# First loads on another queue, and one shared place for the rows of conditional slots, in a fused attention and expert kernel

## The chip, the cores and the metric

The kernel runs on one core of a Trainium2 chip. The metric is device time in microseconds (us), lower is better. Before the change the median of six runs is 837.75 us (835.44 to 839.51).

The core has five engines, each with its own in-order instruction queue: TensorE (PE; its weight loads are shown as PEld), VectorE (DVE), ScalarE (ACT), GpSimd (POOL) and SyncE (SP). Transfers between HBM and on-chip memory are issued from the queues of SP, ACT or POOL and carried out by 16 DMA engines which all three share.

## The reference

The first part is an attention over short windows; its output, laid out as 4608 rows of 512, goes through a layer in which each row is given to one of eight experts.

```python
# attention: q, k, v of shape (8, 8, 576, 64); heads 0-3 plain, 4-7 dilated by 4
scores = scale * np.matmul(q, k.transpose(0, 1, 3, 2))
rel = pos[:, None] - pos[None, :]
mask_plain = (rel >= 0) & (rel < window)                       # window 32
mask_dil = (rel >= 0) & (rel < window * dilation) & (rel % dilation == 0)
scores = np.where(masks[None, :, :, :], scores, -1000000000.0)
scores = scores - np.max(scores, axis=-1, keepdims=True)
attn = np.exp(scores)
attn = attn / (np.sum(attn, axis=-1, keepdims=True) + 1e-09)
x = (attn @ v).transpose(0, 2, 1, 3).reshape(4608, 512)
# experts: w_gate (512, 8), w1 (8, 512, 1024), w2 (8, 1024, 512)
logits = x @ w_gate
expert_idx = np.argmax(logits, axis=1)
gate_w = softmax(logits)[np.arange(N), expert_idx]
# for the rows of expert e:
h = np.maximum(x_sorted[lo:hi] @ w1[e], 0.0)
y_sorted[lo:hi] = h @ w2[e]
out = gate_w[:, None] * y          # rows back in their first order
```

## The kernel before

**Attention** runs as 32 units: for each of the 8 batches, two kinds of heads (`ty` 0 plain, 1 dilated), and two pairs of heads (`hl`) of each kind. Unit 0 is batch 0, plain, first pair; units 0 and 1 use the plain heads' q and k, units 2 and 3 the dilated heads' (the last q and k load of a batch), unit 4 begins batch 1. A unit goes through these steps, pipelined over the units:

- `turn` (L297): PE transposes q and k of the unit (L315 for plain, L323 for dilated heads); VectorE evicts q with its scale, ACT copies k into `kT` (L308).
- `front` (L344): in the first four batches the masks enter by PE: four matmuls of the mask table against a 64x64 identity ("turn") put the mask values into the score banks (L352), and 36 matmuls of q and k add the scores on top (L364). VectorE takes the minima (L380). In later batches VectorE adds the masks ("add0", "add1") instead.
- `exponentials` (L397): ACT, 18 activations (L401). `norm` (L411): VectorE's reciprocal, and POOL's multiply of the whole unit (L416).
- `weights` (L420): PE transposes the weights, VectorE evicts. `summed` (L432): PE multiplies with v (L441). `row_part` (L523): PE transposes back into rows by `turner` (L534), which holds four copies of a 128x128 identity, each with 8 columns of `w_gate` beside it, so that the logits come with the transpose. POOL writes the token numbers into the rows from the constants `cst` (L527).

The `route` of a batch (L546) picks the experts and writes the batch's rows to a bucket in HBM by POOL's indirect DMAs (L227).

**The experts' part** (`moe`, L1092) goes over slots of up to 128 rows of one expert. A slot takes 64 matmuls with w1 (L1173), 16 with w2 (L1205), an eviction by ACT that scales by the gate weight (L1216), a copy of the rows' token numbers (L1219), and an indirect DMA by POOL to the output rows (`scatter`, L1222). 36 slots are sure (`SURE`); the 37th to the 41st (slots 36 to 40) run only if the routing needs them, each within a `tc.If` (L1122). Of these one runs with the data here. Slots are spread between the units of attention by a clock kept while the program is written, and fill the rest of the time alone.

The order on each engine is laid by a scheduler from modelled times; instructions of one engine may change places if their data allow it.

**The first loads.** SP's queue issues q of batch 0 (L255, L261), then v (L270 to L286), and, from L481 on, one write to the bucket and the loads of batch 1. ACT's queue issues an identity (L187), k of batch 0 in four pieces and one load for the dilated heads (L255, L261), and between the second and third k piece the table of all masks (`masks`, L257, 616 KB) and the constants (`cst`, L258, 165 KB); behind k come three more copies of the identity (L474) and `w_gate` (L475) for `turner`.

**The ends of the conditional slots.** `spare` (L1110 to L1116) gives each of the five conditional slots a place of its own for 128 rows and their token numbers. VectorE clears the rows and sets each token number to `NOWHERE`, which the indirect DMA drops. A slot that runs fills its place; behind all blocks (L1238 and after) five `scatter`s write all five places. The write of a sure slot waits in the list `late` until the next slot has made its first eviction.

Of the kernel before, what the change touches and what calls it, by code (L numbers as in the profile page):

```python
# [12 lines left out]
F32 = mybir.dt.float32  # L13
I32 = mybir.dt.int32
BF16 = mybir.dt.bfloat16
# [5 lines left out]
B, H, S, DH = 8, 8, 576, 64  # L21
WIN, DIL = 32, 4
STRIP = S // DIL
N, DM, E, F = B * S, H * DH, 8, 1024
# [11 lines left out]
QUARTER = DM // 4  # L36
# [24 lines left out]
NSLOT = _most_slots()  # L61
NROWS = E * CAP + 128
NOWHERE = 1.0e6
E1 = E + 1
SURE = N // 128
# [8 lines left out]
LAG = 2  # L74
# [9 lines left out]
def _constants():  # L84


    def band(j, ty):

        qi, ki = 64 * j + np.arange(64)[:, None], max(0, 64 * j - WIN) + np.arange(96)[None]
        seen = (qi - ki >= 0) & (qi - ki < WIN)  # L90
        if ty:
            seen &= qi // STRIP == ki // STRIP
        return np.where(seen, 0.0, BIG)

    def mask(ty):

        pairs = [(0, 1), (2, 3), (4, 5), (6, 7), (8, 8)]
        return np.concatenate([np.concatenate([band(j, ty) for j in two]) for two in pairs], 1)

    p = np.arange(128)  # L100
    e = np.arange(E)

    parts = {"add0": mask(0)[:, 0:384], "add1": mask(1)}
    for name, ty, js in (
        ("even0", 0, (0, 2, 4, 6, 8, 8)), ("even1", 1, (0, 2, 4, 6, 8)), ("odd1", 1, (1, 3, 5, 7, 8))
    ):
        parts[name] = np.tile(np.concatenate([band(j, ty) for j in js], 1), (2, 1))
    parts["turn"] = np.tile(np.eye(64), (2, 1))  # L110
    mask_at, n = {}, 0
    for name, a in parts.items():
        mask_at[name] = n
        n += a.shape[1]
    mask_at["odd0"] = mask_at["even0"] + 96
    exact = np.concatenate(list(parts.values()), 1).astype(np.float32).astype(ml_dtypes.bfloat16)
    parts = {
        "tri": np.triu(np.ones((128, 128)), 1)[:, :96],
        "ones": np.ones((128, 128)),
        "rev": np.tile(E - e, (128, 1)),  # L120
        "ecap": np.tile(e * CAP, (128, 1)),
        "tok": p[:, None] + TT * np.arange(NT)[None],
        "row": p[:, None],
        "eidx": np.tile(np.minimum(np.arange(E1), E - 1), (128, 1)),
        "twice": np.tile(2 * np.arange(NSLOT), (128, 1)),
    }
    parts["first"] = np.tile(np.append(np.arange(E)[::-1] / E, -1e6), (128, 1))

# [24 lines left out]
    last_at, k = {}, 0  # L153
    for name, a in last.items():
        last_at[name] = (k, a.size)
        k += a.size
    last = np.concatenate([a.reshape(1, -1) for a in last.values()], 1).astype(np.float32)
    return np.ascontiguousarray(np.concatenate(cols, 1)), at, np.ascontiguousarray(exact), mask_at, np.ascontiguousarray(last), last_at


@with_exitstack
def kernel(
# [10 lines left out]
    nc = tc.nc  # L173
    packed, at, exact, mask_at, packed_last, last_at = _constants()
# [10 lines left out]
    eye = nc.inline_tensor(np.eye(128, dtype=np.float32), name="c_id").ap()  # L185
    ident = turner[:, 0, 0:QUARTER]
    nc.scalar.dma_start(ident, eye)  # L187
    masks = cpool.tile([128, exact.shape[1]], BF16, name="masks")
    cst = cpool.tile([128, packed.shape[1]], F32, name="cst")

    before = cpool.tile([TT, B * NT + 1, E], F32, name="before")
# [6 lines left out]
    avail = cpool.tile([128, E1], F32, name="avail")  # L198
    nc.vector.memset(avail[:, E:E1], 4.0 * NSLOT)
    exs = cpool.tile([1, NSLOT], F32, name="exs")  # L200

    def const(name, rows=128):
        a, w = at[name]
# [46 lines left out]
    def load_qk(b, ty):  # L250
        for name, src, queue in (("q", q, nc.sync), ("k", k, nc.sync if b else nc.scalar)):
            if ty == 0:
                x = pool.tile([TT, NT, 4, DH], F32, tag=name + "0", name=f"{name}0_{b}", bufs=1)
                for h in range(4):
                    queue.dma_start(x[:, :, h, :], src[b, h].rearrange("(t p) d -> p t d", p=TT))  # L255
                    if (b, name, h) == (0, "k", 1):
                        queue.dma_start(masks, nc.inline_tensor(exact, name="c_mask").ap())  # L257
                        queue.dma_start(cst, nc.inline_tensor(packed, name="c_pack").ap())  # L258
            else:
                x = pool.tile([72, 4, 512], F32, tag=name + "1", name=f"{name}1_{b}", bufs=1)  # L260
                queue.dma_start(x, src[b, 4:8].rearrange("h (p x) d -> p h (x d)", p=72))  # L261
            t[b, name, ty] = x
# [81 lines left out]
    def front(qT, kT, ty, early):  # L344
# [3 lines left out]
        for r in range(2) if early else ():  # L348
            rows = slice(DH * r, DH * r + DH)
            for c in range(2):  # L350
                a, n = mask_at[("even", "odd")[c] + str(ty)], 480 if c == r else 384
                nc.tensor.matmul(  # L352
                    sc[r][64 * c : 64 * c + 64, 0:n],
                    lhsT=masks[rows, mask_at["turn"] : mask_at["turn"] + 64],
                    rhs=masks[rows, a : a + n],
                    start=True,
                    stop=False,
                )
# [19 lines left out]
        for i, n, p0, p1, s in places:  # L378
            if early:
                nc.vector.tensor_reduce(  # L380
                    out=lo[p0:p1, i : i + n], in_=s.rearrange("p (i k) -> p i k", k=96),
                    axis=AX, op=OP.min,
                )
            else:
                a = mask_at[f"add{ty}"] + 96 * (1 if (i, ty) == (4, 0) else i % 5)
                nc.vector.tensor_tensor(
                    out=e[p0:p1, i : i + n].rearrange("p i k -> p (i k)"),
                    in0=s,
                    in1=masks[p0:p1, a : a + 96 * n],
                    op=OP.add,  # L390
                )
        if not early:
# [74 lines left out]
    def attention():  # L467


        units = [(b, ty, hl) for b in range(B) for ty in range(2) for hl in range(2)]  # L470
        for ty in range(2):
            load_qk(0, ty)
        for c in range(1, 4):
            nc.scalar.dma_start(turner[:, c, 0:QUARTER], eye)  # L474
        nc.scalar.dma_start(  # L475
            turner[:, :, QUARTER:PART], moe_w_gate.rearrange("(c p) e -> p c e", p=128)
        )
        for ty in range(2):
# [613 lines left out]
    def moe():  # L1092
# [7 lines left out]
            nc.vector.tensor_copy(xt, ps)  # L1100
            return xt

        late, outs, spare = [], [], {}
        xt = None
        for j in range(NSLOT):
            if j == SURE:


                for i in range(SURE, NSLOT):
                    a = pool.tile([128, S], F32, tag="xT", name="spare", bufs=3) if i < SURE + 3 \  # L1110
                        else pool.tile([128, 9, 96], F32, tag="e", name="spare", bufs=LAG + 1)
                    if i >= SURE + 3:
                        a = a.rearrange("p i k -> p (i k)")
                    spare[i] = a[:, 0:DM], mpool.tile([128, 1], I32, name=f"to_{i}", bufs=1)
                    nc.vector.memset(spare[i][0], 0.0)
                    nc.vector.memset(spare[i][1], int(NOWHERE))  # L1116
            if j >= SURE:

                while late:
                    late.pop(0)()  # L1120
                guards.close()
                guards.enter_context(tc.If(live[0] > j))  # L1122
            x = xs[j]
            if xt is None:
                xt = across(j)
# [71 lines left out]
            for f in range(8):  # L1197
# [10 lines left out]
                    fetch()  # L1208
                if f < 7:
                    yield 0.88  # L1210
            if j >= SURE:
                y, to = spare[j]
            else:
                y = mpool.tile([128, DM], F32, tag="yo", name="y")
                to = mpool.tile([128, 1], I32, tag="to", name="to", bufs=6)
# [14 lines left out]
                tc.declare_no_dep(i, group="out", reason="no token is in two slots")  # L1230
                tc.add_to_no_dep_group("out", i)

            (late if j < SURE else outs).append(scatter)
            done[1] = 2 * j + 2
            fetch()
            xt = nxt
            yield 0.88
        guards.close()  # L1238
        for scatter in outs:
            scatter()  # L1240

# [85 lines left out]
```

## Time and profile before

The profiled execution took 839.54 us, with a span from first to last instruction of 837.8 us.

| | value |
|---|---|
| median of 6 runs | 837.75 us |
| the profiled execution, its span | 839.54 us, 837.8 us |
| PE busy | 768.6 us (92%) |
| VectorE, ACT, POOL busy | 288.9, 227.3, 147.6 us |
| mean granted clock of PE | 0.957 |
| DMA over the span | 196.89 MB, mean 235 GB/s |
| w1 matmuls (L1173), w2 matmuls (L1205) | 276.0, 255.1 us |
| last matmul ends, last eviction by ACT | 821.8, 822.5 us |

The profile's own page gives each engine's busy time, the span in 40 slices of 20.9 us, the chain of work that ended last, and groups of like instructions. In timelines a line holds start and duration in us, the engine (a "q" behind its name marks its sequencer, which issues DMAs and waits), the line of the kernel, the operation, what it writes and reads, how many, and in brackets how long the engine had been idle and what released it. Lines on one source line give counts, then shortest, median and longest duration in ns, then first and last start in us. Lines on waits give the total in us, how often, and the longest. A line for a window gives its bounds and length, each engine's busy us and count, PE's granted clock, the DMA engines' share, and GB/s.

### The profile page before, as it was taken

What the parts mean: (1) busy time and instruction counts of PE and PEld (TensorE: products, weight loads), DVE (VectorE), ACT (ScalarE), POOL (GpSimd) and SP (SyncE); (2) the same over time, 40 slices, a digit from 0 to 9 for tenths busy, and PEclk for the clock granted to TensorE, in tenths of its full rate; (3) what the DMA queues carried; (4) which work ended last, traced back from release to release, by engine and by line L of the source; (5) the groups of instructions that cost most, each with busy time, mean ns of one, the idle gap of its engine ahead of it and who ended that gap; (6) DMA issues with size and microseconds to landing.
All of it is one profiled execution on the core that took longest, in us unless ns stands there. A gap on an engine that the chain in (4) does not pass through costs nothing.

```text
span 837.8 us, 17999 instructions
## 1 busy us (share of the span) xinstructions
PE 768.6 (92%) x6822; PEld 588.3 (70%) x6822; DVE 288.9 (34%) x963; ACT 227.3 (27%) x853; POOL 147.6 (18%) x141
## 2 busy tenths in 40 slices
PE   2898888699999999989999998699999999999992
PEld 1787777677877777777777786486867465577770
DVE  1575857557434433443346224611110110101010
ACT  0875655353433233313333110000101001010000
POOL 0233243123121311141113004200000000000002
PEclk9997978899999999999999999699999999999996
DMA  9876669799998984889326728599994393983994
GB/s 202 174 140 166 139 179 385 194 241 293 310 335 259 361 205 151 287 303 276 122 69 211 261 96 291 187 325 320 322 341 144 118 306 110 326 310 128 321 331 161
DMA packets 166268, 196.89 MB, mean 235 GB/s; under 512 B 73569, under 2 KB 88033, under 8 KB 166179
## 3 DMA queue, kind: packets, MB, share of 16 engines
q1 hardware_dynamic: 153156, 169.45, 66.8%
q0 software_dynamic: 6992, 20.35, 6.5%
q10 hardware_dynamic: 6030, 5.89, 2.6%
q8 instruction: 57, 0.93, 0.5%
q14 instruction: 33, 0.26, 0.1%
HBM read 216.98 MB, written 23.33 MB: 287 GB/s over the span
## 4 chain that ended last, share of the span: by engine, by line
PE 85%; issue 4%; ACT 3%; DMA 2%; DVE 2%; SPq 1%; POOL 0%; POOLq 0%; ACTq 0%; DVEq 0%
PE ph L1173 30%; PE py L1205 28%; PE xrow L534 5%; PE xo L441 4%; PE weights L426 4%; PE scores L364 3%; DMA k<-in_k_dram 2%; PE turned L315 2%; PE xt L1098 2%; ACT e L401 2%; PE ph L1135 2%; PE py L1135 2%; PE turned L323 2%; SPq L255 1%; DVE lo L380 1%
## 5 line engine op out<-in xcount | busy, mean ns | idle before, releaser
L1173 PEld LDWEIGHTS ph<-xt,w 128*128 128x128 f32 x2240 | 266.3, 195 | 29.8 <-issue 29.4
L1173 PE MATMUL ph<-xt,w 128*128 128x128 f32 x2240 | 276.0, 279 | 12.2 <-issue 12.2
L1205 PE MATMUL py<-w,h 128*128 128x512 f32 x560 | 255.1, 598 | 0.0
L1205 PEld LDWEIGHTS py<-w,h 128*128 128x128 f32 x560 | 101.5, 191 | 101.9 <-issue 100.2
L1222 POOL DMA_INDIRECT out_dram<-y,to x36 | 35.7, 993 | 365.0 <-ACT y L1216 337.7
L1100 DVE COPY xt<-xt 128x512 f32<-128x512 f32 x38 | 26.2, 689 | 186.1 <-PE xt L1098 183.8
L416 POOL TENSOR_TENSOR e<-e,rec 128x864 f32<-128x864 f32 x32 | 52.4, 1639 | 184.1 <-DVE rec L415 127.9
L1216 ACT ACTIVATE y<-py,x 128x512 f32<-128x512 f32 x36 | 24.7, 686 | 218.0 <-PE py L1205 180.8
L227 POOL DMA_INDIRECT bucket<-rows,idx x48 | 44.6, 930 | 89.7 <-DVE idx L612 31.8
L428 DVE COPY eT<-weights 96x384 f32<-96x384 f32 x96 | 48.5, 547 | 29.6 <-PE weights L426 26.6
L401 ACT ACTIVATE e<-e,lo 128x96 f32<-128x96 f32 x144 | 51.8, 361 | 17.1 <-DVE lo L393 17.1
L1184 ACT ACTIVATE h<-ph 128x512 f32<-128x512 f32 x35 | 20.9, 596 | 127.2 <-PE ph L1173 84.3
L401 ACT ACTIVATE e<-scores,lo 128x96 f32<-128x96 f32 (+1 forms) x160 | 52.9, 344 | 5.0 <-DVE lo L380 2.2
L534 PE MATMUL xrow<-turner,xT 128*96 128x136 f32 x384 | 53.5, 292 | 0.0
L534 PEld LDWEIGHTS xrow<-turner,xT 128*96 128x96 f32 x384 | 49.6, 173 | 5.2 <-issue 4.1
L441 PE MATMUL xo<-eT,v 96*64 96x64 f32 (+1 forms) x1216 | 45.8, 228 | 5.2 <-issue 4.9
L441 PEld LDWEIGHTS xo<-eT,v 96*64 96x64 f32 x1216 | 40.2, 141 | 12.5 <-issue 6.3
L1193 DVE TENSOR_SCALAR h<-ph 128x512 f32<-128x512 f32 x35 | 24.1, 689 | 66.6 <-PE ph L1173 66.5
L426 PE MATMUL weights<-turner,e 128*96 128x128 f32 x288 | 42.7, 299 | 0.8 <-POOL e L416 0.8
L364 PEld LDWEIGHTS scores<-kT,qT 64*64 64x64 f32 x1152 | 30.5, 138 | 15.2 <-issue 6.6
L541 DVE COPY rows<-xrow 96x408 f32<-96x408 f32 x32 | 18.5, 577 | 64.7 <-PE xrow L534 61.4
L364 PE MATMUL scores<-kT,qT 64*64 64x96 f32 x1152 | 35.0, 254 | 5.4 <-ACT kT L308 4.5
(205 smaller groups left out, 594.6 us busy)
## 6 DMA issues: line engine op xcount, KB each, us to landing
w<-in_moe_w_dram SPq DMA_DIRECT2D x164, 1024.0 KB
x<-bucket SPq DMA_DIRECT2D x26, 273.0 KB
v<-in_v_dram SPq DMA_DIRECT2D x32, 192.0 KB
q<-in_q_dram SPq DMA_DIRECT2D x32, 144.0 KB
q<-in_q_dram SPq DMA_DIRECT2D x8, 576.0 KB
v<-in_v_dram SPq DMA_DIRECT2D x48, 96.0 KB
k<-in_k_dram SPq DMA_DIRECT2D x28, 144.0 KB
k<-in_k_dram SPq DMA_DIRECT2D x7, 576.0 KB
```

Source lines behind the costliest of these rows:

```text
L227: nc.gpsimd.indirect_dma_start(out=bucket, out_offset=bass.IndirectOffsetOnAxis(ap=idx, axis=0), in_=rows, in_offset=None, bounds_check=NR ...
L364: nc.tensor.matmul(sc[r][64 * c : 64 * c + 64, 96 * (i % 5) : 96 * (i % 5) + 96], lhsT=qT[rows, 64 * j : 64 * j + 64], rhs=kT[rows, first_ ...
L401: nc.scalar.activation(out=e[p0:p1, i], in_=s[:, 96 * (i - i0) : 96 * (i - i0) + 96], func=AF.Exp, bias=lo[p0:p1, i : i + 1], scale=-1.0, ...
L416: nc.gpsimd.tensor_tensor(out=e, in0=e, in1=rec.unsqueeze(2).broadcast_to([128, 9, 96]), op=OP.mult)
L426: nc.tensor.transpose(tp[0:96, 128 * i : 128 * i + 128], e[:, a + i], ident)
L428: nc.vector.tensor_copy(eT, tp[0:96, 0:384])
L441: nc.tensor.matmul(xo[DH * h : DH * h + DH, at0 : at0 + nq], lhsT=vt[:, 2 * hl + r, j, :] if ty == 0 else vt[:, hl, j, DH * r : DH * r + D ...
L534: nc.tensor.matmul(ps[0:TT, PART * n : PART * n + PART], lhsT=xT[:, TT * (i + n) : TT * (i + n) + TT], rhs=turner[:, c], start=True, stop= ...
L1135: nc.tensor.matmul(out[mine], lhsT=lhsT[:, mine], rhs=ws[:, (j + (g >= KIND[mixed[j]])) % 2, c, cols], start=c == 0, stop=c == n - 1,)
L1173: nc.tensor.matmul(ph[:, fi], lhsT=w1[:, c, 128 * f : 128 * f + 128], rhs=xt[:, c], start=c == 0, stop=c == 3,)
L1205: nc.tensor.matmul(py, lhsT=h[:, f], rhs=w2[:, f], start=f == 0, stop=f == 7)
L1222: i = nc.gpsimd.indirect_dma_start(out=out, out_offset=bass.IndirectOffsetOnAxis(ap=to, axis=0), in_=y, in_offset=None, bounds_check=N - 1 ...
```

## The change

It has two parts.

The masks are split into three tiles, by use: "turn" with "even0" (640 columns), "even1" with "odd1" (960) and "add0" with "add1" (864). These, `cst`, the three further identities and `w_gate` are loaded by POOL's queue rather than ACT's: the first piece ahead of all q and k loads in the program, the others behind these.

The conditional slots share one place, `staged`, with the last sure slot (35). The write of each slot from 35 on is issued at the start of the next slot's block, within its `If`, and the one that is left is issued behind all blocks. No place is cleared any more.

```diff
+    exact, mask_at = [], {}
+    for names in (("turn", "even0"), ("even1", "odd1"), ("add0", "add1")):
...
+    masks = [cpool.tile(list(a.shape), BF16, name=f"masks{i}") for i, a in enumerate(exact)]
...
+    def load_masks(i):
+        nc.gpsimd.dma_start(masks[i], nc.inline_tensor(exact[i], name=f"c_mask{i}").ap())
+
+    def mask(name, rows, n, skip=0):
+        i, a = mask_at[name]
+        return masks[i][rows, a + skip : a + skip + n]
...
                 for h in range(4):
                     queue.dma_start(x[:, :, h, :], src[b, h].rearrange("(t p) d -> p t d", p=TT))
-                    if (b, name, h) == (0, "k", 1):
-                        queue.dma_start(masks, nc.inline_tensor(exact, name="c_mask").ap())
-                        queue.dma_start(cst, nc.inline_tensor(packed, name="c_pack").ap())
...
-                    lhsT=masks[rows, mask_at["turn"] : mask_at["turn"] + 64],
-                    rhs=masks[rows, a : a + n],
+                    lhsT=mask("turn", rows, 64),
+                    rhs=mask(("even", "odd")[c] + str(ty), rows, n),
...
+        load_masks(0)
         for ty in range(2):
             load_qk(0, ty)
+        load_masks(1)
+        nc.gpsimd.dma_start(cst, nc.inline_tensor(packed, name="c_pack").ap())
+        load_masks(2)
         for c in range(1, 4):
-            nc.scalar.dma_start(turner[:, c, 0:QUARTER], eye)
-        nc.scalar.dma_start(
+            nc.gpsimd.dma_start(turner[:, c, 0:QUARTER], eye)
+        nc.gpsimd.dma_start(
             turner[:, :, QUARTER:PART], moe_w_gate.rearrange("(c p) e -> p c e", p=128)
         )
...
-            if j == SURE:
-                for i in range(SURE, NSLOT):
-                    a = pool.tile([128, S], F32, tag="xT", name="spare", bufs=3) if i < SURE + 3 \
-                        else pool.tile([128, 9, 96], F32, tag="e", name="spare", bufs=LAG + 1)
...
-                    nc.vector.memset(spare[i][0], 0.0)
-                    nc.vector.memset(spare[i][1], int(NOWHERE))
+            if j == SURE - 1:
+                staged = pool.tile([128, S], F32, tag="xT", name="staged", bufs=3)
+                staged = staged[:, 0:DM], mpool.tile([128, 1], I32, name="to_staged", bufs=1)
             if j >= SURE:
+                guards.close()
+                guards.enter_context(tc.If(live[0] > j))
                 while late:
                     late.pop(0)()
-                guards.close()
-                guards.enter_context(tc.If(live[0] > j))
...
-            if j >= SURE:
-                y, to = spare[j]
+            if j >= SURE - 1:
+                y, to = staged
...
-            (late if j < SURE else outs).append(scatter)
+            late.append(scatter)
...
         guards.close()
-        for scatter in outs:
-            scatter()
+        late.pop()()
```

More of the change, by code (lines that the diff above doesn't have):

```diff
@@ L110, in _constants @@
     parts["turn"] = np.tile(np.eye(64), (2, 1))
[L111 to L116, printed above, removed]
+    exact, mask_at = [], {}
+    for names in (("turn", "even0"), ("even1", "odd1"), ("add0", "add1")):
+        n = 0
+        for name in names:
+            mask_at[name] = len(exact), n
+            n += parts[name].shape[1]
+        some = np.concatenate([parts[name] for name in names], 1).astype(np.float32)
+        exact.append(np.ascontiguousarray(some.astype(ml_dtypes.bfloat16)))
+    mask_at["odd0"] = mask_at["even0"][0], mask_at["even0"][1] + 96
     parts = {
@@ L157, in _constants @@
     last = np.concatenate([a.reshape(1, -1) for a in last.values()], 1).astype(np.float32)
-    return np.ascontiguousarray(np.concatenate(cols, 1)), at, np.ascontiguousarray(exact), mask_at, np.ascontiguousarray(last), last_at
+    return np.ascontiguousarray(np.concatenate(cols, 1)), at, exact, mask_at, np.ascontiguousarray(last), last_at
 @with_exitstack
@@ L187 @@
     nc.scalar.dma_start(ident, eye)
-    masks = cpool.tile([128, exact.shape[1]], BF16, name="masks")
+    masks = [cpool.tile(list(a.shape), BF16, name=f"masks{i}") for i, a in enumerate(exact)]
     cst = cpool.tile([128, packed.shape[1]], F32, name="cst")
@@ L350, in front @@
             for c in range(2):
-                a, n = mask_at[("even", "odd")[c] + str(ty)], 480 if c == r else 384
+                n = 480 if c == r else 384
                 nc.tensor.matmul(
                     sc[r][64 * c : 64 * c + 64, 0:n],
-                    lhsT=masks[rows, mask_at["turn"] : mask_at["turn"] + 64],
-                    rhs=masks[rows, a : a + n],
+                    lhsT=mask("turn", rows, 64),
+                    rhs=mask(("even", "odd")[c] + str(ty), rows, n),
                     start=True,
@@ L384, in front @@
             else:
-                a = mask_at[f"add{ty}"] + 96 * (1 if (i, ty) == (4, 0) else i % 5)
+                at0 = 96 * (1 if (i, ty) == (4, 0) else i % 5)
                 nc.vector.tensor_tensor(
@@ L388, in front @@
                     in0=s,
-                    in1=masks[p0:p1, a : a + 96 * n],
+                    in1=mask(f"add{ty}", slice(p0, p1), 96 * n, at0),
                     op=OP.add,
@@ L1101, in across @@
             return xt
-        late, outs, spare = [], [], {}
-        xt = None
+        late, xt = [], None
         for j in range(NSLOT):
-            if j == SURE:
-                for i in range(SURE, NSLOT):
-                    a = pool.tile([128, S], F32, tag="xT", name="spare", bufs=3) if i < SURE + 3 \
-                        else pool.tile([128, 9, 96], F32, tag="e", name="spare", bufs=LAG + 1)
-                    if i >= SURE + 3:
-                        a = a.rearrange("p i k -> p (i k)")
-                    spare[i] = a[:, 0:DM], mpool.tile([128, 1], I32, name=f"to_{i}", bufs=1)
-                    nc.vector.memset(spare[i][0], 0.0)
-                    nc.vector.memset(spare[i][1], int(NOWHERE))
+            if j == SURE - 1:
+                staged = pool.tile([128, S], F32, tag="xT", name="staged", bufs=3)
+                staged = staged[:, 0:DM], mpool.tile([128, 1], I32, name="to_staged", bufs=1)
             if j >= SURE:
+                guards.close()
+                guards.enter_context(tc.If(live[0] > j))
                 while late:
                     late.pop(0)()
-                guards.close()
-                guards.enter_context(tc.If(live[0] > j))
             x = xs[j]
```

## The prediction

> **What bounds the kernel now.** I read the page's slices first, for where TensorE (PE) is not busy, and the chain that ended last.
>
> ```profile
> PE   2898888699999999989999998699999999999992
> ...
> PEclk9997978899999999999999999699999999999996
> DMA  9876669799998984889326728599994393983994
> ...
> PE 85%; issue 4%; ACT 3%; DMA 2%; DVE 2%; SPq 1%; POOL 0%; POOLq 0%; ACTq 0%; DVEq 0%
> ```
>
> PE carries 85% of the chain. It is nearly empty in the first slice of 20.9 us and in the last, and between them everything hangs on PE's own progress. So time taken out before PE's first scores, or behind its last matmul, should come out of the whole. The order of the first 30 us on ScalarE (ACT) and PE, from the timeline:
>
> ```profile
> 1.19 1.16 ACTq L255 DMA_DIRECT2D k<-in_k_dram  x2
> 2.38 0.53 ACTq L257 DMA_DIRECT2D masks<-c_mask  x1
> 3.81 0.35 ACTq L258 DMA_DIRECT2D cst<-c_pack  x1
> 5.22 1.03 ACTq L255 DMA_DIRECT2D k<-in_k_dram  x2
> 6.96 0.64 ACTq L261 DMA_DIRECT2D k<-in_k_dram  x1
> 13.21 1.69 ACTq L474 DMA_DIRECT2D turner<-c_id  x3
> 18.63 0.40 ACTq L475 DMA_DIRECT2D turner<-in_moe_w_gate_dram  x1
> 19.06 1.28 ACT L308 ACT_TABLE_LOAD   x1 [19.06 <-DMA k<-in_k_dram]
> 20.36 1.31 ACT L308 COPY kT<-turned 128x288 f32<-128x288 f32 x4
> ```
>
> ```profile
> 7.08 1.19 PE L315 MATMUL turned<-turner,k 96*128 96x96 f32 x6 [1.18 <-DMA k<-in_k_dram]
> 9.28 0.61 PE L352 MATMUL scores<-masks 64*64 64x480 bf16 x4 [1.01 <-DMA masks<-c_mask]
> ...
> 15.29 1.19 PE L315 MATMUL turned<-turner,k 96*128 96x96 f32 x6 [4.25 <-DMA k<-in_k_dram]
> 16.42 0.61 PE L352 MATMUL scores<-masks 64*64 64x480 bf16 x4
> 20.81 3.46 PE L364 MATMUL scores<-kT,qT 64*64 64x96 f32 x72 [3.78 <-ACT kT L308]
> 24.20 1.22 PE L323 MATMUL turned<-turner,q 72*128 72x72 f32 x8
> ```
>
> Unit 0's k is transposed by 8.27 (7.08 + 1.19), yet ACT copies it at 20.36: ACT has first to issue the last of its twelve DMAs, at 18.63. Those issues wait for other transfers. SyncE (SP) shows the same; its own waits hold this line:
>
> ```profile
> SPq L273 <- DMA masks<-c_mask: 2.4, 1, 2.4
> ```
>
> A v load waited for the masks. The q load of SP at 3.50 waited for ACT's identity of 0.76, the eighth issue before it on the two queues together; so the transfers of both take turns on eight completion semaphores, and each issue waits for the transfer eight earlier. Behind that the DMA engines are full, which limits what moving an issue can win:
>
> ```profile
> 0.00:20.00 20.00, 5.88 (x32) 3.97 (x32) 2.73 (x17) 0.94 (x1) 0.65 (x6) 1.00 1.01 204
> ```
>
> DMA share 1.01 at 204 GB/s over the first 20 us (the last two columns). At the end, GpSimd's (POOL's) row in the timeline and two lines of what the kernel's closing line does:
>
> ```profile
> 822.77 0.97 POOL L1222 DMA_INDIRECT out_dram<-spare,to  x1 [13.48 <-ACTq L1121]
> ...
> 827.89 0.98 POOL L1222 DMA_INDIRECT out_dram<-spare,to  x1 [0.30 <-issue]
> ```
>
> ```profile
> L1325 POOLq DRAIN  x3: 51/113/11152, 825.7 to 837.4; - x3
> L1325 SPq DRAIN  x3: 7/7/13, 831.9 to 837.1; - x3
> ```
>
> Five conditional writes, 1.28 us apart, though only the first spare holds rows (there is one write into a spare by ACT, at 821.81). POOL's drain begins at 825.72 and lasts 11.15 us, to 836.87: 8.0 us after the last write ends at 828.87. SP, the next latest, drained at 831.9.
>
> **The head, step by step.** Six issues leave ACT's queue (masks, cst, three identities, gate). What stays is ident, four k pieces, and the last k load. By the eight-transfer rule the last waits for a transfer issued before 1.2 us, which lands by about 5 (cst and the third k piece were released so at 3.81 and 5.22), so ACT is free at about 6 to 7, its table load (1.28) ends by 8.3, and its first copy then waits for PE's transposed k. That needs the second k piece, landed at 6.94 before; the first mask piece (640 of 2464 columns, 160 of 616 KB) now travels beside it. I add 1 us: transposed at 9.3, scores 0.45 us after the copy starts (20.36 to 20.81), so at 9.8 to 10.4. **Ceiling of the gain: 20.81 - 10.4 = 10.4 us.**
>
> Nothing is removed from what the DMA engines carry, only the order changes, and three queues now share them. So the fourth k piece (landed 15.2: PE's wait at 15.29) and the last k load (landed by 18.6: the gate's issue waited for it) hardly come sooner. Two places are held by them. If PE keeps its order, unit 1's transposes stand before unit 0's scores: 15.2 + 1.2 + 0.7 = 17.1, **a gain of 3.7 us, the floor.** If scores go first, unit 2's k transposes (25.21 before) cannot start before 18.6: **a gain of 6.6 us.** The engine orders are laid by a scheduler from modelled times (POOL's L527 of a later unit runs before L416 of unit 0), and ACT free early favours scores first. I take 6.0, near the second; 3.7 and 10.4 bound it.
>
> The gain carries: from 38.7 on the chain runs on PE. The next loads, q and k of batch 1, were issued at 27.64 to 32.1 behind SP's v loads, and unit 4 transposes at 44.24, so there is slack for 6 us but not much over 10. The 5.57 us stall at 152.77 (transposes of q waiting for DMA) sits behind weight loads that the routing starts, so it moves along with PE.
>
> What moves to POOL: eight DMA issues. No plain load by POOL is in this trace; the nearest row is the indirect write, 1.28 us each, so 8 x 1.28 = 10.2, free at about 11; the landing row is 827.89 to 830.54, 2.7 us. First mask piece: 0.8 + 2.7, under contention 4 to 6, ahead of 9.28: cost nothing. Queued behind the issues are L527 (11.69 before, waits for cst, now the third issue; needed when rows are written at about 39) and L416 (27.55, now about 21.5): covered by 10 us. If the gate's 512 short rows took four times as long, POOL would be free at 15, still covered. A gain below nothing is not to be had from work that is covered; the costly end is in the rivals.
>
> The Trainium skill speaks against this move: "DMA: Bandwidth & Descriptors", section "SWDGE vs HWDGE vs iDMA", has plain loads issued by SP or ACT, since GpSimd builds descriptors in software, and its section on the anatomy of a DMA gives about 2.0 us plus bytes over 436 GB/s, an estimate of 2.4 us for the first piece, landing at 3.2. "SBUF — State Buffer", section "Who interferes with whom", adds that VectorE in some modes keeps GpSimd from writing descriptors; VectorE is busy 2.73 of the first 20 us here. By either the sum would stay as it is, as the piece is wanted only at 9.
>
> Mask reads from three tiles and the changed column offsets alter no instruction: nothing.
>
> **The tail.** Removed: ten memsets on VectorE (five of 485 ns at 453 to 505, five of 59 ns at the start) under PE work, 0 (at most 0.8, the one wait PE had on a spare). Slot 35's write moves into the block of slot 36; it was issued at 808.32, 13.5 us idle before it, and must land (814.9) before ACT writes the shared place at 821.8: covered by 7 us. Removed: four writes, 4 x 1.28 = 5.1. Added: the one write must wait until ACT has stepped through the skipped blocks, 823.42 (its last event there) instead of 822.5: about 1.0. So it starts at 823.8, ends 824.8, and a drain 8.0 behind it ends at 832.8, a gain of 4.1. SP at 831.99 caps the gain at 4.9. If the drain hangs on something other than the last write, the gain is 0; a loss I exclude, since stepping through the skipped blocks takes ACT 1.6 us in all (821.81 to 823.42) and four writes are 5.1. I take **4.1**, by the drain row.
>
> **Sum.** 6.0 + 4.1 = 10.1. The profiled execution took 839.54, span 837.8; that gives a span of 827.7 and 829.4 for it. The median shown, 837.75, lies 1.8 below that execution, so **827.6 us**.
>
> **Rivals.**
> *PE's scores go first and k lands sooner than I allow.* ACT's k no longer queues behind 616 KB of masks in its own ring. Against: DMA share 1.01. Head 10.4, tail 4.9: 822.4.
> *The head stays DMA-bound, only one end pays.* PE keeps its order (3.7) and the drain pays little, or the tail pays alone. For: share 1.01, the row at 15.29. 837.75 - 4.1 = 833.6.
> *Nothing measurable:* the drain is not behind the writes and the first scores wait for the last load anyway: 837.
> *Slower: POOL's queue becomes the head's wait.* The first mask piece gates every score and L416 gates the weights. PE now wants the masks at 9.3; each us the piece lands after that eats the head. It decides when the piece lands after about 9.3 + 11.5 + 4.1 = 25, or when eight issues take over (27.55 + 4.1)/8 = 4 us each, three times the row. With five us each POOL is free at 41, norm 13 us late, less the tail: 847. Against: 1.28 us in every POOL row; for: no cold POOL load in the trace.
>
> **How the numbers follow.** Forecast (824 to 831) 0.50; both ends pay fully 0.18; one end 0.19; nothing 0.05; POOL 0.08. The clock adds noise: granted 0.65 from 136 to 144 us and 0.57 from 152 to 160, and the runs lie from 835.4 to 839.5. About 0.3%, 2.5 us, is what a measurement tells from no change: faster 0.87, same 0.05, slower 0.08. The forecast's own range is 824 to 831; reaching both faster-side rivals gives 820.5 to 834.
>
> **What would show it.** ACT's table load near 7 instead of 19.06; first scores between 10 and 17; whether unit 1's transposes still precede them; unit 2's wait on k near 19; POOL's eight issues done by 12; one write of the shared place at about 824 in the old clock, and POOL's drain 8 us after it or SP as the last. Wrong would be: a mask wait on PE beyond 12 us, a POOL drain unmoved, or a lost 6 us reappearing before 160 us.

## The result, and the profile after

The changed kernel takes 832.74 us (median of 20 runs, 830.53 to 835.8), the kernel before beside it 836.92 us (46 runs). The ratio is 0.9945 with a 95% interval of 0.9933 to 0.9956: a gain of 4.6 us (3.7 to 5.6), where 10.1 was forecast. The direction is as forecast and the gain is less than half. The time lies outside the forecast's own range, 824 to 831, and inside the wider one that also reaches the two faster rivals, 820.5 to 834.

The profiled execution took 831.29 us, its span 829.5. That is 8.3 us below the span of before, nearly twice what the medians say: the profiled execution of before lay 2.6 us above the median beside it, this one 1.5 below. A profile of the same changed kernel in a later group of runs has a span of 832.2. So one pair of profiles shows well what waits for what, and badly how much the whole gained; sizes are taken from the medians below. In two of the four groups of runs below the kernel before measured about 808 us, in the others 837, so only ratios to the kernel before of the same group are compared.

The same slices, the chain and the first window of the profile after:

```profile
PE   4888887799999999989999998699999999999993
...
PEclk9998888899999999999999999799999999999997
DMA  9877679899998984889326728599994393983995
...
PE 84%; issue 4%; DMA 3%; ACT 2%; SPq 2%; DVE 2%; another core or an unknown queue 1%; POOL 0%; POOLq 0%; DVEq 0%; ACTq 0%
```

```profile
0.00:20.00 20.00, 7.68 (x84) 6.24 (x88) 3.01 (x13) 2.88 (x5) 5.35 (x14) 1.00 0.97 203
```

PE's first slice went from 2 to 4 tenths, the last from 2 to 3. The DMA engines are as full as they were in the first 20 us (0.97 at 203 GB/s against 1.01 at 204). In the chain DMA went from 2% to 3% and SP's queue from 1% to 2%; new in it are SP's issues of batch 1's q and k, from 27.75 us on, and the landing of that k at 35.22. The timeline of the head after, ACT and POOL first:

```profile
1.18 2.63 ACTq L266 DMA_DIRECT2D k<-in_k_dram  x4
5.71 0.55 ACTq L269 DMA_DIRECT2D k<-in_k_dram  x1
6.30 1.28 ACT L316 ACT_TABLE_LOAD   x1 [6.30 <-DMA k<-in_k_dram]
10.14 0.88 ACT L316 COPY kT<-turned 128x288 f32<-128x288 f32 x2 [2.57 <-PE turned L323]
```

```profile
1.26 1.30 POOL L207 DMA_DIRECT2D masks<-c_mask  x2 [0.80 <-POOLq L1316]
2.55 0.54 POOL L483 DMA_DIRECT2D cst<-c_pack  x1
3.08 0.54 POOL L207 DMA_DIRECT2D masks<-c_mask  x1
3.61 1.60 POOL L486 DMA_DIRECT2D turner<-c_id  x3
5.19 0.77 POOL L487 DMA_DIRECT2D turner<-in_moe_w_gate_dram  x1
```

ACT is free at 6.30 instead of 19.06 and copies its first k at 10.14 instead of 20.36. POOL issues its eight loads in 4.7 us, 0.5 to 0.8 us each. PE in the same stretch:

```profile
9.40 1.19 PE L323 MATMUL turned<-turner,k 96*128 96x96 f32 x6 [2.92 <-DMA k<-in_k_dram]
10.52 0.61 PE L360 MATMUL scores<-masks 64*64 64x480 bf16 x4
11.06 1.22 PE L323 MATMUL turned<-turner,q 96*128 96x96 f32 x6
16.40 1.20 PE L323 MATMUL turned<-turner,k 96*128 96x96 f32 x6 [4.12 <-DMA k<-in_k_dram]
17.52 0.61 PE L360 MATMUL scores<-masks 64*64 64x480 bf16 x4
17.85 3.49 PE L372 MATMUL scores<-kT,qT 64*64 64x96 f32 x72
...
35.36 0.69 PE L323 MATMUL turned<-turner,k 96*128 96x96 f32 x6 [1.30 <-DMA k<-in_k_dram]
```

Two things are to be seen. Unit 0's k is ready for scores at 10.6, but unit 1's transposes still stand ahead of unit 0's scores on PE and wait till 16.40 for their k, so the scores come at 17.85 against 20.81: 3.0 us sooner. And at unit 4, the first unit of batch 1, there is a wait that was not there before: 1.30 us for that batch's k. It had been issued by SP, behind the v loads of batch 0:

```profile
23.46 3.45 SPq L294 DMA_DIRECT2D v<-in_v_dram  x7
27.02 0.38 SPq L493 DMA_DIRECT2D bucket<-blank  x1
27.50 2.21 SPq L266 DMA_DIRECT2D q<-in_q_dram  x4
29.81 3.48 SPq L266 DMA_DIRECT2D k<-in_k_dram  x4
```

Its four k issues begin at 29.81. Before, they began at 29.88 (the first of the four is shown), and unit 4's transposes of q and k stood at 37.42 and 37.92, with no wait for a load:

```profile
29.88 0.78 SPq L255 DMA_DIRECT2D k<-in_k_dram  x1
```

```profile
37.42 0.66 PE L315 MATMUL turned<-turner,q 96*128 96x96 f32 x6
37.92 0.41 PE L315 MATMUL turned<-turner,k 96*128 96x96 f32 x3
```

PE came sooner, SP's queue did not. At the end of the kernel, the remaining write and the drains:

```profile
818.04 0.97 POOL L1227 DMA_INDIRECT out_dram<-staged,to_staged  x1 [14.41 <-ACTq L1243]
```

```profile
L1329 POOLq DRAIN  x3: 51/109/10860, 817.8 to 829.2; - x3
L1329 SPq DRAIN  x3: 7/7/13, 825.7 to 828.9; - x3
```

POOL's drain ends at 828.67, 9.66 us behind the end of the last write (8.0 before), and is still the last engine: SP had drained at 825.7.

Five points in time of both profiles (us). What the head has ahead at 63 us (3.4) is about what it has ahead at 185 us (3.8); the rest up to 5.7 comes between 250 and 560 us, at places the change doesn't touch.

| | before | after |
|---|---|---|
| first scores (L364, L372) | 20.81 | 17.85 |
| first matmul of the first routing (the "first rank matmul" of the expectations) | 63.43 | 60.07 |
| first eviction of an expert slot by ACT | 185.05 | 181.24 |
| last eviction by ACT starts | 821.81 | 816.14 |
| end, and its distance from that eviction | 837.77, 15.96 | 829.52, 13.38 |

### The profile page after: what moved, and what is told of

It reads as the page before. It is cut to its first block, busy times and chain, and to the rows that moved or that the text cites. A ratio compares the mean times of both kernels' runs of the same rounds, so it can differ in the third digit from the quotient of the medians.

```text
span 829.5 us, 17991 instructions
## 1 busy us (share of the span) xinstructions
PE 764.7 (92%) x6822; PEld 585.5 (71%) x6822; DVE 287.0 (35%) x953; ACT 227.4 (27%) x853; POOL 147.9 (18%) x145
## 4 chain that ended last, share of the span: by engine, by line
PE 84%; issue 4%; DMA 3%; ACT 2%; SPq 2%; DVE 2%; another core or an unknown queue 1%; POOL 0%; POOLq 0%; DVEq 0%; ACTq 0%
PE ph L1178 30%; PE py L1210 28%; PE xrow L546 5%; PE xo L449 4%; PE weights L434 3%; PE scores L372 3%; DMA k<-in_k_dram 3%; PE turned L323 2%; PE xt L1110 2%; SPq L266 2%; PE ph L1140 2%; PE py L1140 2%; ACT e L409 2%; PE turned L331 1%
## 5 line engine op out<-in xcount | busy, mean ns | idle before, releaser
L409 ACT ACTIVATE e<-e,lo 128x96 f32<-128x96 f32 x144 | 51.8, 361 | 16.6 <-DVE lo L401 16.6
L449 PEld LDWEIGHTS xo<-eT,v 96*64 96x64 f32 x1216 | 40.3, 141 | 12.3 <-issue 6.9
L553 DVE COPY rows<-xrow 96x408 f32<-96x408 f32 x32 | 18.5, 577 | 65.6 <-PE xrow L546 62.3
L316 ACT COPY kT<-turned 128x288 f32<-128x288 f32 x64 | 23.4, 410 | 61.5 <-PE turned L323 31.7
L372 PEld LDWEIGHTS scores<-kT,qT 64*64 64x64 f32 x1152 | 30.8, 138 | 11.2 <-issue 6.7
```

Of the source, the lines that this page charges most:

```text
L372: nc.tensor.matmul(sc[r][64 * c : 64 * c + 64, 96 * (i % 5) : 96 * (i % 5) + 96], lhsT=qT[rows, 64 * j : 64 * j + 64], rhs=kT[rows, first_ ...
L409: nc.scalar.activation(out=e[p0:p1, i], in_=s[:, 96 * (i - i0) : 96 * (i - i0) + 96], func=AF.Exp, bias=lo[p0:p1, i : i + 1], scale=-1.0, ...
L449: nc.tensor.matmul(xo[DH * h : DH * h + DH, at0 : at0 + nq], lhsT=vt[:, 2 * hl + r, j, :] if ty == 0 else vt[:, hl, j, DH * r : DH * r + D ...
```

## The experiments

Each run is given as its ratio to the kernel before of the same group, with its 95% interval.

### Each end by itself

The change's loads with the spares of before, and the reverse:

```diff
 # the loads alone: spares and writes of before
-        late.pop()()
+        for scatter in outs:
+            scatter()
...
 # one place alone: first loads of before
-        load_masks(0)
...
+                    if (b, name, h) == (0, "k", 1):
+                        queue.dma_start(masks, nc.inline_tensor(exact, name="c_mask").ap())
```

> The loads of the change with the five spare places of before. Theory: the head is worth about 3 us (first scores at 17.9 instead of 20.8, and PE reaches the k of batch 1 when it has not landed yet, so that the rest stays behind SP's loads): ratio to the kernel before about 0.9965, the tail in the trace as before (POOL's drain ends about 8 us behind the last write). Rival, that the whole of the measured 4.6 us is the tail's: 1.000. Rival, that it is all the head's: 0.9945.

> One shared place and one last write, with the loads of before. Theory: about 2 to 2.6 us, the difference between 15.99 us (before) and 13.36 us (after) from the start of ACT's last eviction to the end of the span: ratio about 0.997. As predicted, with a drain 8 us behind the last write: 4.1 us, 0.995. Rival: nothing, 1.000. In the trace, first scores at 20.8 as before.

The loads alone gave 1.0000 (0.9977 to 1.0022), the shared place alone 0.9946 (0.9926 to 0.9967). Measured so, the tail pays the whole gain of the change and the head nothing; the theories ahead of the two runs, 0.9965 and 0.997, were both off. To see whether the head's zero was chance, it was run again in two other groups, and the change once more:

> The change's loads with the five places and five writes of before, once more. If the head pays nothing to speak of: ratio to before 0.998 to 1.001. If its first result was an effect of that group of runs, and the head pays the 3 us by which the scores come sooner: ratio 0.996 to 0.997.

> The change's loads with the tail of before a third time, beside the three others. Ratio 0.998 to 1.001 if SP's queue or the clock takes the head's gain; 0.996 to 0.997 if the two results before were chance.

> The changed kernel itself, beside those below. Theory (the tail pays 4.4 us, the head 0 to 1.5): ratio 0.993 to 0.9955, as the result. Rival, that both parts add up from their traces (3.3 and 3.5): 0.9915.

The head gave 1.0005 (0.9985 to 1.0025) and 1.0012 (0.9991 to 1.0033), the change 0.9947 (0.9927 to 0.9967). Three times out of three the head is worth nothing that can be measured, though its first scores stand at 18.0 to 18.7 us in the three profiles, against 20.81 before.

A part of it is lost at the other end of the kernel. POOL's last drain in the third of these runs, and in the kernel before with only some v loads moved (it comes below, under SP's queue), which has the same five writes:

```profile
L1337 POOLq DRAIN  x3: 51/109/11793, 793.4 to 805.8; - x3
```

```profile
L1326 POOLq DRAIN  x3: 51/113/11152, 793.8 to 805.5; - x3
```

In all five profiles with the change's loads and five writes of before, the drain ends 8.66 us behind the last write's end, and the span ends 16.6 us behind the start of the last eviction; in both with the loads and writes of before it is 8.01 and 16.0. So the change's loads cost 0.6 us at the end. Why the drain is longer then is not shown.

### The tail: is it the writes?

Four dropped writes put back behind the last one, and the last one left out (the output then lacks the rows of the last slot that runs):

```diff
 # five writes
-        late.pop()()
+        last = late.pop()()
+        for i in range(4):
...
+            nc.vector.memset(none[1], int(NOWHERE))
+            with tc.issue_after(last):
+                scatter(*none)
 # no last write
-        late.pop()()
```

> The change, with four more writes behind the last one whose token numbers are all dropped, as before had them. Theory (the tail is paid by the four writes that went, and the last drain follows the last write): the last write starts about 5.1 us later, POOL's drain ends 3 to 5 us later, time 3 to 5 us above the change, ratio to before 0.998 to 1.001. Rival (what pays is the waiting and clearing of the spares, not the writes): time as the change's, ratio 0.9945.

> The change without its one write behind all blocks: the rows of the last live slot are left out of the output. Theory, that POOL's drain has a length of its own, 9 to 11 us from where it starts, whatever it follows: the end moves by less than 1 us. Rival, the prediction's, that the drain ends 8 us behind the last write's end: the drain then starts behind the 36th slot's block and SP becomes the last engine, the whole 2 to 3 us shorter than the change.

Four more writes cost all that the change won: 1.0012 (0.9994 to 1.0030), which is 0.0065 or 5.4 us above the change's 0.9947 from another group. Their rows in the timeline, and POOL's and SP's drains without the last write:

```profile
818.54 0.97 POOL L1227 DMA_INDIRECT out_dram<-staged,to_staged  x1 [14.41 <-ACTq L1244]
819.81 0.97 POOL L1227 DMA_INDIRECT out_dram<-none,none  x1 [0.30 <-issue]
...
823.64 0.97 POOL L1227 DMA_INDIRECT out_dram<-none,none  x1 [0.30 <-issue]
```

```profile
L1328 POOLq DRAIN  x3: 51/103/8242, 813.4 to 827.1; - x3
L1328 SPq DRAIN  x3: 7/7/13, 826.4 to 826.8; - x3
```

The writes are 1.28 us apart, as before. Without the last one, POOL's drain still lasts 8.24 us but ends at 821.7, and SP is the last engine at 826.4: 0.9908 (0.9885 to 0.9931), 3.3 us below the change in the same group. So the rival came, in which SP becomes the last engine, and not the theory that the end hardly moves. From the start of the last eviction to the end there are 9.8 us with no write, 11.7 to 14.8 (mean 12.9) in the nine profiles of kernels with one, and 16.0 to 17.5 (mean 16.5) in the eight of kernels with five. Of the nine, 11.7 is the shared place alone; with the change's loads none is below 12.2. So the tail hangs on the writes, and the one that remains still costs some 3 us.

### The head: scores sooner

Two ways to bring the scores forward, with all else as the change has it. In the first, POOL's loads from the second mask piece on wait until the fourth k piece has landed; in the second, unit 1's k transposes go behind unit 0's scores:

```diff
 # held loads
+        seen = cpool.tile([1, 1], F32, name="seen")
+        landed = nc.gpsimd.tensor_copy(seen, t[0, "k", 0][0:1, 0, 3, 0:1])
+        with tc.issue_after(landed.ins):
             load_masks(1)
...
 # scores first
-                    qT[n] = turn(b2, ty2, hl2, n)
+                    with ExitStack() as order:
+                        if i == 0 and n == "k":
+                            order.enter_context(tc.issue_after(t["score"].ins))
+                        qT[n] = turn(b2, ty2, hl2, n)
```

> The change, with POOL's second and third mask piece, the constants, the identities and the gate weights issued only when the fourth k piece has landed (POOL reads one element of it first). Theory, that POOL's large packets push the k pieces back: the second k piece is there at about 7.5 instead of 9.3, the fourth at about 13 to 14 instead of 16.3, first scores at about 15; but the whole gains less than 1 us over the change, since PE then waits longer for the k of batch 1 (1.3 us now, 3 to 4 then). Rival, that only the transfer's total counts: the fourth k piece lands at 16 as in the change.

> The change, with unit 1's transposes of k put behind unit 0's scores on PE. Theory, that the k of batch 1 on SP's queue caps the head (landed at 35.2, wait of 1.3 us on PE): unit 0's scores at about 10.8 instead of 17.9, yet the time within 1 us of the change, the wait at unit 4's transposes growing to 2 to 5 us. Rival, the prediction's own, that PE's order holds the head and that the loads of batch 1 have slack: 3 us or more below the change, ratio about 0.991.

With POOL's loads held, PE no longer waits for unit 1's k:

```profile
7.85 1.20 PE L323 MATMUL turned<-turner,k 96*128 96x96 f32 x6 [1.76 <-DMA k<-in_k_dram]
...
10.55 1.19 PE L323 MATMUL turned<-turner,k 96*128 96x96 f32 x6
...
12.00 2.57 PE L372 MATMUL scores<-kT,qT 64*64 64x96 f32 x72
...
31.25 1.20 PE L323 MATMUL turned<-turner,q 96*128 96x96 f32 x6 [2.53 <-DMA q<-in_q_dram]
33.97 1.20 PE L323 MATMUL turned<-turner,k 96*128 96x96 f32 x6 [1.52 <-DMA k<-in_k_dram]
```

The second k piece, transposed at 9.40 in the change, goes at 7.85, the fourth at 10.55 instead of 16.40. So POOL's loads had delayed k. Fewer bytes beside it and shorter packets would both do that; these runs don't part the two. From the packets that the trace lists between 4 and 6 us of the changed kernel:

```
queue     packets   KB   share of 16 engines' time   median packet
POOL's         73  279   0.58                        5120 B, 220 ns
SP's          464  117   0.26                        256 B, 18 ns
ACT's         423  105   0.26                        256 B, 18 ns
```

POOL's median packet takes 220 ns where those of q and k take 18, and POOL's queue got over half of the engines' time. The Trainium skill's "DMA: Bandwidth & Descriptors", section "Queues, rings and completion order", says that each engine goes round the queues and changes only at the end of a packet. The table shows no single turns; one of these packets for one would give POOL 0.86 (220 of 220 + 18 + 18), and the counts are six of SP's and six of ACT's to each of POOL's. The same page's section "SWDGE vs HWDGE vs iDMA" gives up to 4096 B as the preferred packet; here the median is 5120 B, four mask rows of 1280 B, and the largest 5760 B, three of 1920 B.

Yet neither version gained: 0.9968 (0.9945 to 0.9991) and 0.9961 (0.9936 to 0.9987), no better than the tail alone in the same group (0.9946). Scores stand at 12.0 and 12.3, 5.9 and 5.5 us ahead of the change's, and the time came back by unit 4: waits of 2.53 and 1.52 us in the rows above, 0.85 and 1.80 with scores first. Its k transposes stand at 33.97 and 34.97, only 1.4 and 0.4 us ahead of the change's. What they wait for comes by SP's queue.

### SP's queue

SP issues 13 v loads of batch 0's dilated heads, which units 2 and 3 need, before q and k of batch 1. They were moved behind these:

```diff
-        for ty in range(2):
-            load_v(0, ty)
+        load_v(0, 0)
...
                 if hl2 == 1 and b2 + 1 < B:
                     load_qk(b2 + 1, ty2)
+                if i == 0:
+                    load_v(0, 1)
```

First with the change's tail: v later alone, with scores first, with held loads too, and with only the loads from the third on held:

> The change, with the thirteen v loads of batch 0's dilated heads behind q and k of batch 1 in SP's queue, PE's order as the change has it. Theory (SP's queue caps the head: what PE won at its first scores it gives back waiting for batch 1's k at unit 4): no wait at unit 4, first rank matmul 0.8 to 1.5 us sooner than the change's 60.1 to 61.1, time 0 to 1.5 us below the change's, ratio to before 0.9925 to 0.9947. Rival (the cap costs nothing, the rest of the lost head gain is the granted clock alone): the wait goes, the first rank matmul and the time stay as the change's, ratio 0.9945 to 0.9955. Rival (v of the dilated heads is now late): a wait on v at units 2 or 3 longer than 1 us, ratio above 0.996.

> The change with two orders altered: unit 0's scores ahead of unit 1's transposes of k on PE, and on SP's queue the 13 v loads of the dilated heads behind q and k of batch 1. Theory, that SP's queue caps the head: no wait over 0.3 us at unit 4's transposes (0.9 and 1.8 us with the scores first alone), first route's rank matmul at about 57 to 58 instead of 60, and 2 to 3 us below the change. Rival, that whatever the head wins is given back before the experts' part: the same time as the change within 1 us.

> The kernel above with POOL's later loads held until the fourth k piece has landed. Theory: fourth k piece at about 12 to 13, unit 4's transposes 2 to 4 us sooner again, first rank matmul at about 56, 3 to 5 us below the change. Rival: no more than the kernel above, as the mask piece for the dilated units now lands last and holds unit 2.

> The version with scores first and v later, with POOL's loads from the third on held until the fourth k piece has landed; the first two mask pieces are not held. If the mask wait of 2.5 us at unit 2 was all that spoiled the version that held all of them, the first scores stand at 10 to 11, PE has no mask wait at unit 2, and the time is 1 to 2 us below the version without holding, ratio to before 0.987 to 0.989. Rival (the second mask piece, sent early, delays k as it did in the change): first scores at 12 and ratio 0.990.

They gave 0.9919 (0.9895 to 0.9943), 0.9899 (0.9878 to 0.9919), 0.9914 (0.9893 to 0.9935) and 0.9891 (0.9865 to 0.9918), all below the change's 0.9945; the intervals of the second and the fourth lie apart from the change's. In none did PE wait for q or k at unit 4. Holding every load made the second mask piece late:

```profile
19.99 0.58 PE L360 MATMUL scores<-masks,masks 64*64 64x480 bf16 x4 [2.52 <-DMA masks<-c_mask]
```

With that piece not held the wait is gone and the first scores stand at 11.2, but the expected further gain isn't to be told from the version without holding. These two, 0.0101 and 0.0109 of 837 or 8.5 and 9.1 us below before, are the fastest kernels found.

Then the head alone, with the tail of before throughout, which tells a cap in SP's queue from a gain that v later brings by itself:

> The kernel before, with nothing but the thirteen v loads of batch 0's dilated heads behind batch 1's q and k in SP's queue. If SP's queue is a cap that binds only once PE's head is sooner: first scores at 20.8, no gain, ratio 0.999 to 1.001. If fewer transfers beside the first ones pay by themselves: first scores sooner by 1 us or more, ratio 0.997 to 0.998.

> The change's loads with the tail of before, and v later. If SP's queue takes the head's gain: with the cap gone the 2 to 3 us of the first scores stay, ratio 0.9965 to 0.9975, against 1.000 with v first. If the granted clock takes it: ratio 0.999 to 1.001 as with v first, and a lower mean clock than before's.

> As the one before, and PE's transposes of unit 1's k behind unit 0's scores. If PE's order was the rest of what the forecast of 6.0 us lacked: first scores at 12 to 13, ratio 0.992 to 0.995. If the granted clock gives back whatever comes sooner: ratio 0.997 or more.

| loads | v | scores | ratio to before | first scores, us | mean clock (before 0.9725) |
|---|---|---|---|---|---|
| before's | later | as before | 1.0004 (0.9984 to 1.0024) | 20.6 | 0.9718 |
| change's | first | as before | 1.0012 (0.9991 to 1.0033) | 18.0 | 0.9700 |
| change's | later | as before | 0.9968 (0.9953 to 0.9984) | 18.5 | 0.9709 |
| change's | later | first | 0.9953 (0.9930 to 0.9977) | 12.8 | 0.9722 |

Neither the loads nor v later pays by itself; both together gain 0.32%, and their interval lies apart from that of the loads alone. SP's queue in the second row's kernel, and the wait that follows:

```profile
19.51 7.90 SPq L294 DMA_DIRECT2D v<-in_v_dram  x13
27.52 0.38 SPq L493 DMA_DIRECT2D bucket<-blank  x1
28.01 2.35 SPq L266 DMA_DIRECT2D q<-in_q_dram  x4
30.45 4.23 SPq L266 DMA_DIRECT2D k<-in_k_dram  x4
```

```profile
36.24 0.69 PE L323 MATMUL turned<-turner,k 96*128 96x96 f32 x6 [1.77 <-DMA k<-in_k_dram]
```

and in the third row's:

```profile
20.59 3.01 SPq L266 DMA_DIRECT2D q<-in_q_dram  x4
23.70 2.77 SPq L266 DMA_DIRECT2D k<-in_k_dram  x4
26.51 7.46 SPq L294 DMA_DIRECT2D v<-in_v_dram  x13
```

```profile
35.05 0.41 PE L323 MATMUL turned<-turner,k 96*128 96x96 f32 x3
```

With v behind, k of batch 1 is issued 6.75 us sooner and unit 4 starts on it with no wait.

**What stays open.** That the order in SP's queue decides whether the loads pay is shown; by which wait is shown in part. The wait that v later removes is 1.77 us in that profile, 0.75 and none in the other two of the loads alone, and the gain is 3.6 us (0.0044 of 808; by the two intervals, an estimate, 1.5 to 5.7). In the profiles of the second and third rows 0.4 us of it stand at the first matmul of the first routing (60.95 and 60.57) and 2.1 at the last eviction (789.49 and 787.40). Part may be the clock: the loads alone ran at a mean clock 0.0014, 0.0030 and 0.0025 below before's in their three groups, and over the 36 runs of that kernel 0.001 of clock goes with 0.5 to 0.7 us (the slope in each group; in the runs of before beside them it is 0.2 to 0.5). By its own slopes that makes 1.0 to 1.5 us. In the profile without a wait at unit 4 PE came there late: 36 score matmuls took 1.87 us instead of 1.04, and the granted clock was 0.74 from 25 to 45 us, against 0.91 before. No experiment set the clock, so this share is not shown. Nor is what scores first adds to v later: 0.9953 and 0.9968 overlap, as 0.9899 and 0.9919 do, and 0.9953 lies between the two forecasts made for it.

## Why the prediction missed

**ACT's queue: right.** Free at 6 to 7 was said, 6.30 it is. The turn about on eight completions holds: the last k load was issued at 5.71, when the first k piece had landed (5.69). Unit 0's k was to be transposed by 9.3, its second piece landing 1 us later than before; it landed 2.3 us later, and the transposes run from 9.40 to 10.59.

**POOL's issues as cover: right, at a lower price.** Eight at 1.28 us were to end at about 11; they ended at 5.96. The first mask piece was to land at 4 to 6; it landed at 5.77, and no score waited for it. Nothing of the rival in which POOL's queue becomes the head's wait was seen. What the prediction lacked was not POOL's time but its transfers': it said that the fourth k piece hardly comes sooner, and it came 1.15 us later (16.31 against 15.16), as the second did (9.26 against 6.94).

**"I take 6.0": wrong, this is the first step that failed.** The prediction gave a floor of 3.7 if PE kept its order, 6.6 if scores went first, and chose near the second because the scheduler would favour it. PE kept its order. First scores 17.85, a gain of 2.96: the floor less 0.74 for the later k.

**"The gain carries … there is slack for 6 us but not much over 10": wrong, the second step that failed.** The prediction read unit 4's transposes at 44.24. Those are unit 5's; unit 4's stand at 37.42 for q and 37.92 for k in the trace of before. The k piece they need landed at 35.02, so the slack was 2.9 us. In the changed kernel it landed at 35.22 and PE stood there till 35.36. So even a head of 6 us would not have carried: held loads and scores first brought the scores forward by 8 us and more and gained nothing over the tail alone. With v behind, the loads gained 2.6 us (0.0032 of 808), and with scores first too, 8.0 us sooner than before, 3.8; so 6.0 was too much even without this cap. The head's term of the sum, 6.0, measured 0.0 (−1.8 to +1.9, from the first of its three runs). That the time still lies inside the wider range is no merit of this term.

**The tail's 4.1: right.** Alone it measured 0.0054 of 808, 4.4 us (2.7 to 6.0); in its profile the last write ends 3.17 us behind the start of the last eviction and the drain 7.68 later. In the changed kernel the last write ends 2.87 us behind the start of the last eviction, 3.0 was said, and 7.06 it had been. Its drain follows by 9.66 and, in the second profile, 9.17 instead of 8.0: that the drain grows longer with the change's loads is not in the sum. SP, which was to cap the gain at 4.9, did not come into play.

**The rivals.** What happened is the second one, with its number: the tail pays alone, 833.6 forecast, 832.74 measured, at a chance of 0.19. It stood there for the right reason in part ("PE keeps its order") but with a DMA-bound head as its cause; what took the head's gain is in good part an issue queue, at 30 us.

## What to carry to other kernels

Before a gain at the start is carried to the end, look for the next place where the engine meets a transfer that another queue issues, and read the slack there from that transfer's landing to its first use; here it was 2.9 us, and two changes that each paid nothing gained 0.32% together. A write by an indirect DMA behind the last work costs its 1.28 us each even if all its rows are dropped, so the last writes are to be counted. Where three queues feed the same DMA engines, loads moved to one can hold up those of another: here the second and fourth k pieces landed 2.3 and 1.15 us later.

## What was not expected of the hardware

POOL's final drain lasts 8.2 us even with its last write 8.4 us past (804.07 + 0.97 to 813.44), and ends 9.7 us after the last write in the changed kernel. A plain load by POOL takes 0.5 to 0.8 us of its time to issue, against 1.28 us from one indirect write to the next. The mask and constant loads by POOL travelled in packets of 3456 to 5760 B that join two to four rows, q and k of the plain heads by SP and ACT in packets of 256 B. With the loads of the change the final drain ends 8.66 us behind the last of five writes, with those of before 8.01.
